# FFT mixing and a squared-ReLU FFN on one core: x cast one period ahead, first loads uncast on one queue, first transform over six PSUM banks

## Chip, core and metric

One core of a Trainium2 chip runs one program. The metric is device time in microseconds (us) of one execution; smaller is better.

## What is computed

x is 8 x 3008 x 256 in fp32. Along the 3008 positions each channel is transformed (real FFT), multiplied by a complex filter of 1504 + 1 frequencies per channel, and transformed back. The 24064 rows that come out go through a squared-ReLU FFN with 2048 hidden columns:

```python
X = np.fft.rfft(x, axis=1)
y = np.fft.irfft(X * (filt_r + 1j * filt_i)[None], n=3008, axis=1)
h = np.maximum(y.reshape(24064, 256) @ w_in, 0.0)
out = (h * h @ w_out).astype(np.float32)
```

## The kernel before

All matmuls are fp16 with fp32 sums. The FFT of length 3008 = 64 x 47 is done by constant matrices in stages, batch by batch.

- **Load and cast.** `load_x` (L139) brings a quarter of a batch, 96 x 2048 fp32, into one of two buffers; `cast_x` (called in `unit_a`) turns it to fp16 on VectorE (L186) in one of two buffers.
- **Stage A.** `unit_a`, 16 units a batch, four per quarter: one matmul of 512 columns (L196), copied from PSUM by ScalarE (even units, L201) or VectorE (odd, L203). After each quarter 384 KB go to the DRAM scratch dU (L205), in rows of 256 fp16 elements. `read_u` (L213) reads all of dU back in another order, in two transfers.
- **Stages B and P.** `unit_b`, 12 units: two matmuls (L219), and VectorE multiplies with the filter tile sF (L222). `unit_p`: four matmuls (L236), copied by ScalarE (L238); every third unit writes 384 KB to the scratch dZ (L241). `read_z` (L247) reads it back in four transfers.
- **Stage Y.** `unit_y`, 16 units of four matmuls (L259), copied to y by ScalarE or VectorE in turn (L266, L268).
- **FFN.** 47 groups of 512 rows, eight slots each. In a slot `ffn_g1` does the first matmul for two of 16 hidden tiles (L289) and the ReLU on ScalarE (L293), `ffn_g2` an eighth of the second matmul of the group before (L304), `ffn_sq` the square on VectorE (L297). `ffn_out` copies (L311) and stores (L313) a result every fourth slot. h2 (hidden values) has two buffers.

Engines work through their instructions in the order written; SyncE issues nearly all DMAs. That order is written out by hand. `fft_plan(b)` gives each unit of a batch a slot and one of two places in it: stage A in slots 0 to 7, the read of dU after slot 8, B and P in 13 to 25, the reads of z in 27, the loads of the next batch's first two quarters in 28, stage Y in 31 to 38. Batch 0 runs its plan alone, ahead of the FFN (the lead-in). Batch b from 1 to 7 starts its plan at the FFN slot in which the group that needs it lies 40 or 48 slots ahead (slots 0, 40, 88, 136 and so on, one period each), and each slot of the FFN then runs:

```python
ffn_g1(g, k)
run(work, s, 0)        # place 0
ffn_g2(g - 1, k)
run(work, s, 1)        # place 1
ffn_out(g - 1, k)
ffn_sq(g, k)
```

PSUM has eight banks: two for the FFT (`psF`), two tiles of two banks for the FFN's first matmul (`psH`), two for its second.

Constants and weights: sSA comes on SyncE, sSB, sSP and sSY on ScalarE's queue. The filter tile sF and both FFN weights come on GpSimd's queue, cast from fp32 to fp16 by the DMA (L170 to L179). At slot 12 of the lead-in VectorE copies sF's second half (L348, L349).

Of the kernel before, what the change touches and what calls it, by code (L numbers as in the profile page):

```python
# [86 lines left out]
def kernel(  # L87
# [29 lines left out]
    p_x16 = ctx.enter_context(tc.tile_pool(name="p_x16", bufs=2))  # L117
# [14 lines left out]

    def psF(name):
        return pps.tile([128, 512], F32, tag="psF", name=name, bufs=2)
# [4 lines left out]
    def load_x(b, c):  # L139

        t = p_x32.tile([96, 8, D], F32, tag="x32", name=f"x32_{b}_{c}")
# [8 lines left out]

    sSA = const.tile([94, 96], F16, name="sSA")
    nc.sync.dma_start(out=sSA, in_=dSA.ap())
    load_x(0, 0)
    load_x(0, 1)

    sSB = const.tile([128, NC, 128], F16, name="sSB")
    nc.scalar.dma_start(out=sSB, in_=dSB.ap().rearrange("p (a b) -> p a b", b=128))
    sSP = const.tile([128, NC, 2, 128], F16, name="sSP")
    nc.scalar.dma_start(out=sSP, in_=dSP.ap().rearrange("p (a t b) -> p a t b", t=2, b=128))
    sSY = const.tile([96, 94], F16, name="sSY")  # L160
    nc.scalar.dma_start(out=sSY, in_=dSY.ap())
# [3 lines left out]
    nc.gpsimd.memset(sF[32:64, 0, 0, :], 0.0)  # L165
    nc.gpsimd.memset(sF[96:128, 0, 0, :], 0.0)
    for c0, c1 in ((0, 12), (12, 24)):
        for r0, filt in ((0, filt_r), (64, filt_i)):
            v = filt[0:1504, :].rearrange("(k1 k2) d -> k1 k2 d", k2=47)
            nc.gpsimd.dma_start(out=sF[r0:r0 + 32, 0, c0:c1, :], in_=v[:, c0:c1, :])  # L170
            a = max(c0, 1)
            nc.gpsimd.dma_start(out=sF[r0 + 32:r0 + 64, 0, a:c1, :],
                                in_=v[:, 47 - a:47 - c1:-1, :])
    nc.gpsimd.dma_start(out=sF[32:33, 0, 0, :], in_=filt_r[1504:1505, :])

    sWin = const.tile([128, 2, DFF], F16, name="sWin")
    nc.gpsimd.dma_start(out=sWin, in_=moe_w_in.rearrange("(t r) j -> r t j", r=128))
    sWout = const.tile([128, NJT, 256], F16, name="sWout")
    nc.gpsimd.dma_start(out=sWout, in_=moe_w_out.rearrange("(jt r) c -> r jt c", r=128))  # L179
# [9 lines left out]
    def unit_a(b, a):  # L189

        c, i = divmod(a, 4)
        if i == 0:
            cast_x(b, c)
# [10 lines left out]
        if i == 3:  # L204
            nc.sync.dma_start(  # L205
# [3 lines left out]
    def read_u(b):  # L209
        ut = p_ut.tile([128, NC, D], F16, tag="ut", name=f"ut_{b}")  # L210
        v = dU[b].rearrange("(p s) d -> p s d", s=NC)
        for s0, s1 in ((0, 8), (8, 24)):
            nc.sync.dma_start(out=ut[:, s0:s1, :], in_=v[:, s0:s1, :])  # L213
# [102 lines left out]
    def fft_plan(b):  # L316
# [6 lines left out]
        for a in range(16):  # L323
            if a % 4 == 0 and a // 4 + 2 < 4:
                put(a // 2, 0, load_x, b, a // 4 + 2)
            put(a // 2, a % 2, unit_a, b, a)
# [74 lines left out]
```

## Time and profile before

| | |
|---|---|
| median of 3 runs | 897.73 us (896.83 to 898.89) |
| the profiled execution | 898.58 us |
| its span, first to last instruction | 896.80 us |
| lead-in, until the first FFN matmul | 91.47 us |
| TensorE busy | 792.4 us |
| VectorE, ScalarE, GpSimd busy | 479.1, 543.6, 7.9 us |

Times in the rows are us from the span's start unless marked ns. PE is TensorE's matmuls, PEld its weight loads, DVE VectorE, ACT ScalarE, POOL GpSimd, SP SyncE; a name with q (SPq) is the engine's queue issuing a DMA. `out<-in` names tiles; x32 after a shape is a count. An idle time is written with what ended it.

### The profile page before, as it was taken

The numbers are of one execution on the slowest core, as the hardware profiler recorded it, in microseconds if no ns is written. First come the engines' busy times: TensorE is split into PE (matmuls) and PEld (weight loads), VectorE is DVE, ScalarE is ACT, GpSimd is POOL, SyncE is SP. The second block draws the span as 40 slices with busy tenths as digits, with TensorE's granted clock in tenths as the row PEclk, the third lists the DMA queues.
The fourth block names the chain that finished last, engine by engine and source line by source line (L and its number), as shares of the span: only waits on it lengthen the run. The fifth ranks groups of instructions, "written<-read, shape, count | busy, mean of one in ns | idle before, by whom it ended". The sixth has DMA issues, their size and how long they took to land.

```text
span 896.8 us, 14010 instructions
## 1 busy us (share of the span) xinstructions
PE 792.4 (88%) x5952; PEld 552.6 (62%) x5952; DVE 479.1 (53%) x636; ACT 543.6 (61%) x695; POOL 7.9 (1%) x17
## 2 busy tenths in 40 slices
PE   1245799979998899979999799988999799999998
PEld 0023377657776577656776577765767567766666
DVE  1443765566654575456744566545744567443332
ACT  1112667756765667656776566755676567766664
POOL 3000000000000000000000000000000000000000
PEclk9999999999999999999999999999999999999999
DMA  9935533544353426243261433534162432411111
GB/s 243 226 116 148 157 124 126 146 129 141 115 151 99 151 80 182 66 129 130 89 194 43 133 137 122 143 107 152 71 182 65 128 130 89 124 36 37 36 47 49
DMA packets 90942, 107.01 MB, mean 119 GB/s; under 512 B 4296, under 2 KB 81032, under 8 KB 86664
## 3 DMA queue, kind: packets, MB, share of 16 engines
q1 hardware_dynamic: 86384, 100.11, 37.1%
q0 software_dynamic: 4096, 3.64, 2.5%
q10 hardware_dynamic: 400, 2.38, 0.9%
q8 instruction: 46, 0.75, 0.4%
q14 instruction: 16, 0.13, 0.0%
HBM read 59.94 MB, written 49.81 MB: 122 GB/s over the span
## 4 chain that ended last, share of the span: by engine, by line
PE 84%; DVE 6%; DMA 5%; issue 2%; ACT 2%; SPq 0%; DVEq 0%; ACTq 0%
PE psO L304 36%; PE psH L289 34%; PE psP L236 5%; DVE x L186 4%; DMA x<-in_x_dram 4%; PE psA L196 3%; PE psB L219 3%; PE psY L259 3%; DVE h L297 2%; ACT ze L238 1%; ACT h L293 1%; DMA dU<-u 1%; DVE u L203 1%; DMA ut<-dU 0%; DMA zt<-dZ 0%
## 5 line engine op out<-in xcount | busy, mean ns | idle before, releaser
L293 ACT ACTIVATE h<-psH 128x1024 f16<-128x1024 f32 x376 | 385.1, 1024 | 206.0 <-PE psH L289 203.7
L304 PE MATMUL psO<-sWout,h 128*128 128x256 f16 x3008 | 388.6, 272 | 0.0
L289 PE MATMUL psH<-yt,sWin 128*128 128x512 f16 (+7 forms) x1728 | 388.1, 352 | 0.2 <-DVE yt L268 0.2
L297 DVE TENSOR_TENSOR h<-h 128x1024 f16<-128x1024 f16 x376 | 258.0, 686 | 188.8 <-ACT h L293 188.8
L304 PEld LDWEIGHTS <-h 128*128 128x128 f16 x3008 | 291.5, 98 | 83.1 <-issue 6.9
L289 PEld LDWEIGHTS <-sWin 128*128 128x128 f16 x1728 | 159.8, 98 | 100.6 <-issue 2.0
L222 DVE TENSOR_TENSOR prod<-psB,sF 128x1024 f16<-128x1024 f32 x96 | 117.4, 1224 | 57.6 <-PE psB L219 56.6
L196 PE MATMUL psA<-x,sSA 94*96 94x512 f16 x128 | 51.4, 421 | 73.9 <-DVE x L186 72.4
L238 ACT CAST ze<-psP 128x512 f16<-128x512 f32 x96 | 56.2, 585 | 68.0 <-PE psP L236 68.0
L203 DVE CAST u<-psA 96x512 f16<-96x512 f32 x64 | 44.0, 687 | 71.6 <-PE psA L196 70.3
L201 ACT CAST u<-psA 96x512 f16<-96x512 f32 x64 | 36.9, 577 | 57.8 <-PE psA L196 56.8
L268 DVE CAST yt<-psY 128x376 f16<-128x376 f32 x64 | 35.2, 550 | 66.5 <-PE psY L259 66.5
L196 PEld LDWEIGHTS <-sSA 94*96 94x96 f16 x128 | 16.0, 130 | 81.7 <-DVE x L186 59.5
L236 PE MATMUL psP<-prod,sSP 128*128 128x256 f16 x384 | 63.0, 290 | 1.6 <-DVE prod L222 0.9
L311 ACT COPY ost<-psO 128x512 f32<-128x512 f32 x94 | 55.4, 589 | 5.8 <-PE psO L304 5.8
L219 PE MATMUL psB<-ut,sSB 128*128 128x256 f16 x192 | 38.9, 288 | 16.8 <-DMA ut<-dU 10.6
L259 PEld LDWEIGHTS <-zt 96*128 96x128 f16 x512 | 36.7, 102 | 24.6 <-DMA zt<-dZ 6.9
L186 DVE CAST x<-x 94x2048 f16<-94x2048 f32 x32 | 38.9, 1217 | 23.2 <-DMA x<-in_x_dram 23.2
L259 PE MATMUL psY<-sSY,zt 96*128 96x94 f16 x512 | 44.1, 213 | 8.1 <-DMA zt<-dZ 6.5
L236 PEld LDWEIGHTS <-sSP 128*128 128x128 f16 x384 | 39.8, 104 | 9.1 <-issue 1.4
L219 PEld LDWEIGHTS <-sSB 128*128 128x128 f16 x192 | 19.4, 101 | 41.1 <-issue 20.5
L266 ACT CAST yt<-psY 128x376 f16<-128x376 f32 x64 | 29.9, 468 | 10.4 <-PE psY L259 10.4
(16 smaller groups left out, 13.3 us busy)
## 6 DMA issues: line engine op xcount, KB each, us to landing
out_dram<-ost SPq DMA_DIRECT2D x94, 256.0 KB, 2.2
x<-in_x_dram SPq DMA_DIRECT2D x28, 768.0 KB, 9.1
dU<-u SPq DMA_DIRECT2D x32, 384.0 KB, 3.4
dZ<-ze SPq DMA_DIRECT2D x32, 384.0 KB, 2.3
zt<-dZ SPq DMA_DIRECT2D x32, 384.0 KB, 5.8
ut<-dU SPq DMA_DIRECT2D x8, 1024.0 KB, 6.1
ut<-dU SPq DMA_DIRECT2D x8, 512.0 KB, 3.7
x<-in_x_dram SPq DMA_DIRECT2D x4, 640.0 KB, 5.7
```

The lines of the kernel that those rows point to most:

```text
L186: nc.vector.tensor_copy(out=t, in_=x32s.pop((b, c))[0:94])
L196: nc.tensor.matmul(ps[0:96, :], sSA, x16s[(b, c)][:, 2 * i:2 * i + 2, :], start=True, stop=True)
L219: nc.tensor.matmul(ps[:, i * D:(i + 1) * D], sSB[:, 2 * p + i, :], uts[b][:, 2 * p + i, :], start=True, stop=True)
L222: nc.vector.tensor_mul(out=prod, in0=ps.rearrange("p (a d) -> p a d", d=D).unsqueeze(1).to_broadcast([128, 2, 2, D]), in1=sF[:, :, 2 * p:2 ...
L236: nc.tensor.matmul(ps[:, i * D:(i + 1) * D], sSP[:, 2 * p + i, v, :], prod[:, v, i, :], start=(v == 0), stop=(v == 1))
L238: nc.scalar.copy(out=zes[(b, c)][:, 2 * i6:2 * i6 + 2, :], in_=ps.rearrange("p (a d) -> p a d", d=D))
L259: nc.tensor.matmul(ps[:, 94 * jj:94 * jj + 94], zt[:, 4 * (g % 2) + jj, dt * 128:(dt + 1) * 128], sSY, start=True, stop=True)
L289: nc.tensor.matmul(ps[:, i, o:o + n], sWin[:, dt, jt * 128:(jt + 1) * 128], yts[b][:, dt, r:r + n], start=(dt == 0), stop=(dt == 1))
L293: nc.scalar.activation(out=h2[:, 2 * s:2 * s + 2, :], in_=ps, func=AF.Relu)
L297: nc.vector.tensor_mul(out=v, in0=v, in1=v)
L304: nc.tensor.matmul(pso[g][:, t % 2, :], h2s[g][:, jt, t * 128:(t + 1) * 128], sWout[:, jt, :], start=(jt == 0), stop=(jt == NJT - 1))
L311: nc.scalar.copy(out=ost, in_=pso[g])
```

## The change

- x is cast a period ahead: batch b+1's four casts stand in slots 27, 30, 33 and 36 (place 1) of batch b's plan, no longer in stage A; there are four fp16 buffers. The loads of its first two quarters move from slot 28 to slot 22; those of the last two follow the first two casts, in slots 27 and 30, and no longer lie in stage A. Batch 0's casts stay in stage A.
- In the lead-in all four quarters of x are loaded at once, the last two into the FFN's h2 buffers.
- sSB, the filters (as fp32, into the two y buffers), sSP and sSY follow on SyncE in this order; then, at slot 9, both FFN weights as fp32 into the h2 buffers. VectorE casts the filters, GpSimd the weights, in eight copies of 1024 columns.
- In the lead-in the writes of dU and its read go out on ScalarE's queue.
- In the lead-in the FFT's PSUM tiles rotate over six banks: two of `psF` and four of `psH`.

```diff
     p_x32 = ctx.enter_context(tc.tile_pool(name="p_x32", bufs=2))
-    p_x16 = ctx.enter_context(tc.tile_pool(name="p_x16", bufs=2))
+    p_x16 = ctx.enter_context(tc.tile_pool(name="p_x16", bufs=4))
     p_u = ctx.enter_context(tc.tile_pool(name="p_u", bufs=3))
...
+    banks = []
     def psF(name):
-        return pps.tile([128, 512], F32, tag="psF", name=name, bufs=2)
+        if not prologue[0]:
+            return pps.tile([128, 512], F32, tag="psF", name=name, bufs=2)
+        if not banks:
+            for k in range(2):
+                banks.append((pps.tile([128, 512], F32, tag="psF", name=f"{name}_{k}", bufs=2), None))
+            for k in range(2):
+                t = pps.tile([128, 2, 512], F32, tag="psH", name=f"{name}_h{k}", bufs=2)
+                banks.extend([(t, 0), (t, 1)])
+        t, i = banks.pop(0)
+        return t if i is None else t[:, i, :]
+    prologue = [True]
...
-    def load_x(b, c):
-        t = p_x32.tile([96, 8, D], F32, tag="x32", name=f"x32_{b}_{c}")
+    def load_x(b, c, pool=None, tag="x32"):
+        t = (pool or p_x32).tile([96, 8, D], F32, tag=tag, name=f"x32_{b}_{c}")
         if b + 1 < B:
...
     sSA = const.tile([94, 96], F16, name="sSA")
...
     load_x(0, 1)
+    load_x(0, 2, p_h2, "h2")
+    load_x(0, 3, p_h2, "h2")
     sSB = const.tile([128, NC, 128], F16, name="sSB")
-    nc.scalar.dma_start(out=sSB, in_=dSB.ap().rearrange("p (a b) -> p a b", b=128))
-    sSP = const.tile([128, NC, 2, 128], F16, name="sSP")
-    nc.scalar.dma_start(out=sSP, in_=dSP.ap().rearrange("p (a t b) -> p a t b", t=2, b=128))
-    sSY = const.tile([96, 94], F16, name="sSY")
-    nc.scalar.dma_start(out=sSY, in_=dSY.ap())
+    vSB = dSB.ap().rearrange("p (a b) -> p a b", b=128)
+    nc.sync.dma_start(out=sSB, in_=vSB)
     sF = const.tile([128, 2, NC, D], F16, name="sF")
-    nc.gpsimd.memset(sF[32:64, 0, 0, :], 0.0)
-    nc.gpsimd.memset(sF[96:128, 0, 0, :], 0.0)
+    f32s = []
     for c0, c1 in ((0, 12), (12, 24)):
+        t = p_y.tile([128, 12, D], F32, tag="yt", name=f"f32_{c0}")
+        if c0 == 0:
+            nc.gpsimd.memset(t[32:64, 0, :], 0.0)
+            nc.gpsimd.memset(t[96:128, 0, :], 0.0)
         for r0, filt in ((0, filt_r), (64, filt_i)):
             v = filt[0:1504, :].rearrange("(k1 k2) d -> k1 k2 d", k2=47)
-            nc.gpsimd.dma_start(out=sF[r0:r0 + 32, 0, c0:c1, :], in_=v[:, c0:c1, :])
+            nc.sync.dma_start(out=t[r0:r0 + 32, 0:12, :], in_=v[:, c0:c1, :])
             a = max(c0, 1)
-            nc.gpsimd.dma_start(out=sF[r0 + 32:r0 + 64, 0, a:c1, :],
-                                in_=v[:, 47 - a:47 - c1:-1, :])
-    nc.gpsimd.dma_start(out=sF[32:33, 0, 0, :], in_=filt_r[1504:1505, :])
+            nc.sync.dma_start(out=t[r0 + 32:r0 + 64, a - c0:12, :],
+                              in_=v[:, 47 - a:47 - c1:-1, :])
+        if c0 == 0:
+            nc.sync.dma_start(out=t[32:33, 0, :], in_=filt_r[1504:1505, :])
+        f32s.append(t)
+    sSP = const.tile([128, NC, 2, 128], F16, name="sSP")
+    nc.sync.dma_start(out=sSP, in_=dSP.ap().rearrange("p (a t b) -> p a t b", t=2, b=128))
+    sSY = const.tile([96, 94], F16, name="sSY")
+    nc.sync.dma_start(out=sSY, in_=dSY.ap())
     sWin = const.tile([128, 2, DFF], F16, name="sWin")
-    nc.gpsimd.dma_start(out=sWin, in_=moe_w_in.rearrange("(t r) j -> r t j", r=128))
     sWout = const.tile([128, NJT, 256], F16, name="sWout")
-    nc.gpsimd.dma_start(out=sWout, in_=moe_w_out.rearrange("(jt r) c -> r jt c", r=128))
+    def load_w():
+        w32 = p_h2.tile([128, 2, DFF], F32, tag="h2", name="win32")
+        nc.sync.dma_start(out=w32, in_=moe_w_in.rearrange("(t r) j -> r t j", r=128))
+        o32 = p_h2.tile([128, NJT, 256], F32, tag="h2", name="wout32")
+        nc.sync.dma_start(out=o32, in_=moe_w_out.rearrange("(jt r) c -> r jt c", r=128))
+        for k in range(4):
+            nc.gpsimd.tensor_copy(out=sWin[:, :, 512 * k:512 * k + 512],
+                                  in_=w32[:, :, 512 * k:512 * k + 512])
+        for k in range(4):
+            nc.gpsimd.tensor_copy(out=sWout[:, 4 * k:4 * k + 4, :], in_=o32[:, 4 * k:4 * k + 4, :])
+    def cast_f(k):
+        c0, c1 = 12 * k, 12 * k + 12
+        nc.vector.tensor_copy(out=sF[:, 0, c0:c1, :], in_=f32s[k])
+        nc.vector.tensor_copy(out=sF[0:64, 1, c0:c1, :], in_=sF[64:128, 0, c0:c1, :])
+        nc.vector.tensor_copy(out=sF[64:128, 1, c0:c1, :], in_=sF[0:64, 0, c0:c1, :])
...
         if i == 0:
-            cast_x(b, c)
             us[(b, c)] = p_u.tile([96, 8, D], F16, tag="u", name=f"u_{b}_{c}")
...
         if i == 3:
-            nc.sync.dma_start(
+            q = nc.scalar if prologue[0] else nc.sync
+            q.dma_start(
                 out=dU[b].rearrange("(m q) d -> q m d", q=96)[:, 8 * c:8 * c + 8, :],
...
         v = dU[b].rearrange("(p s) d -> p s d", s=NC)
+        q = nc.scalar if prologue[0] else nc.sync
         for s0, s1 in ((0, 8), (8, 24)):
-            nc.sync.dma_start(out=ut[:, s0:s1, :], in_=v[:, s0:s1, :])
+            q.dma_start(out=ut[:, s0:s1, :], in_=v[:, s0:s1, :])
         uts[b] = ut
...
         for a in range(16):
-            if a % 4 == 0 and a // 4 + 2 < 4:
-                put(a // 2, 0, load_x, b, a // 4 + 2)
+            if b == 0 and a % 4 == 0:
+                put(a // 2, 0, cast_x, b, a // 4)
             put(a // 2, a % 2, unit_a, b, a)
...
         if b + 1 < B:
-            put(28, 1, load_x, b + 1, 0)
-            put(28, 1, load_x, b + 1, 1)
+            for c in range(2):
+                put(22, 1, load_x, b + 1, c)
+            for c in range(4):
+                put(27 + 3 * c, 1, cast_x, b + 1, c)
+                if c < 2:
+                    put(27 + 3 * c, 1, load_x, b + 1, c + 2)
         for n in range(16):
...
     for r in range(41):
-        if r == 12:
-            for c0, c1 in ((0, 12), (12, 24)):
-                nc.vector.tensor_copy(out=sF[0:64, 1, c0:c1, :], in_=sF[64:128, 0, c0:c1, :])
-                nc.vector.tensor_copy(out=sF[64:128, 1, c0:c1, :], in_=sF[0:64, 0, c0:c1, :])
+        if r == 9:
+            load_w()
+            cast_f(0)
+            cast_f(1)
         run(plan0, r, 0)
         run(plan0, r, 1)
+    prologue[0] = False
```

## Rows read from the trace of the kernel before

**Rows 1.** The page, chain that ended last, share of the span by engine.

```profile
PE 84%; DVE 6%; DMA 5%; issue 2%; ACT 2%; SPq 0%; DVEq 0%; ACTq 0%
```

**Rows 2.** Stages: length; busy PE, PEld, DVE, ACT, POOL; clock, DMA share, GB/s.

```profile
16.30:41.50 25.20, 8.70 (x16) 2.28 (x15) 9.20 (x12) 4.65 (x8) 1.90 (x2) 1.00 1.16 224
...
51.27:77.25 25.98, 17.56 (x72) 9.85 (x72) 14.60 (x12) 7.03 (x12) 0.00 (x0) 1.00 0.18 73
...
83.07:91.47 8.40, 6.75 (x65) 5.28 (x66) 3.85 (x7) 3.78 (x8) 0.00 (x0) 1.00 1.12 271
91.47:896.80 805.33, 759.43 (x5803) 534.98 (x5800) 446.47 (x601) 526.88 (x666) 0.00 (x0) 1.00 0.37 112
```

**Rows 3.** Waits from 92 to 897 us: us in total, times, longest us.

```profile
PE psA L196 <- DVE x L186: 41.9, 27, 1.7
```

**Rows 4.** Events in order of time, third period: start, us, engine line.

```profile
177.92 0.42 PE L196 MATMUL psA<-x,sSA 94*96 94x512 f16 x1 [1.23 <-DVE x L186]
...
184.15 0.42 PE L196 MATMUL psA<-x,sSA 94*96 94x512 f16 x1 [1.64 <-DVE x L186]
```

**Rows 5.** Chain that ended last, in order of time: start, us, what.

```profile
41.50 6.00 DMA dU<-u
47.65 3.48 DMA ut<-dU
...
79.57 3.46 DMA zt<-dZ
```

**Rows 6.** The page, costliest groups: busy us, mean ns | idle before.

```profile
L293 ACT ACTIVATE h<-psH 128x1024 f16<-128x1024 f32 x376 | 385.1, 1024 | 206.0 <-PE psH L289 203.7
...
L222 DVE TENSOR_TENSOR prod<-psB,sF 128x1024 f16<-128x1024 f32 x96 | 117.4, 1224 | 57.6 <-PE psB L219 56.6
...
L203 DVE CAST u<-psA 96x512 f16<-96x512 f32 x64 | 44.0, 687 | 71.6 <-PE psA L196 70.3
L201 ACT CAST u<-psA 96x512 f16<-96x512 f32 x64 | 36.9, 577 | 57.8 <-PE psA L196 56.8
...
L186 DVE CAST x<-x 94x2048 f16<-94x2048 f32 x32 | 38.9, 1217 | 23.2 <-DMA x<-in_x_dram 23.2
```

**Rows 7.** Stage Y of the second period, slots 31 to 38, as rows 2.

```profile
248.81:265.13 16.32, 16.32 (x160) 11.95 (x159) 8.61 (x16) 12.08 (x18) 0.00 (x0) 1.00 0.56 155
```

**Rows 8.** Events in order of time, second period.

```profile
242.46 2.26 SPq L247 DMA_DIRECT2D zt<-dZ  x4
...
252.77 0.68 DVE L297 TENSOR_TENSOR h<-h 128x1024 f16<-128x1024 f16 x1
...
256.09 0.33 PE L259 MATMUL psY<-sSY,zt 96*128 96x94 f16 x4
```

**Rows 9.** DMA packets, 50 to 53 us, then 87 to 91 us.

```profile
DMA packets 204, 1.29 MB, mean 429 GB/s; under 512 B 18, under 2 KB 18, under 8 KB 76
...
DMA packets 140, 1.02 MB, mean 254 GB/s; under 512 B 16, under 2 KB 16, under 8 KB 16
```

**Rows 10.** DMA queues, 36 to 42, then 10 to 16 us: packets, MB, share.

```profile
q0 software_dynamic: 1221, 0.66, 77.6%
q1 hardware_dynamic: 1225, 0.62, 50.6%
...
q1 hardware_dynamic: 121, 0.86, 57.1%
...
q0 software_dynamic: 117, 0.06, 7.2%
```

**Rows 11.** Chain up to 95 us, two units of stages B and P.

```profile
58.02 0.59 ACT ze L238
...
58.66 0.59 PE psB L219 x2
59.24 0.87 PE psP L236 x4
...
60.77 0.59 PE psB L219 x2
```

## The prediction

> **What bounds the kernel now.** I read the page's chain first, then the span cut into stages, then who waited for whom, then events in order of time. The chain that ended last lies on TensorE for 84% [rows 1]. The cut shows two regimes [rows 2]. Up to 91.47 us the first transform runs alone, and TensorE is busy for 33 us (8.70 + 17.56 + 6.75). In the 805 us after that it is busy for 759, so what it still waits for is time on the path. The list of waits of that stretch names one thing of size: the stage-A matmuls wait 41.9 us in 27 waits for the cast of x on VectorE [rows 3]. One transform in order of time shows the shape: the cast begins when the VectorE queue reaches it, and TensorE stands 1.23 us before the first of its four pieces and 1.64 us before the next [rows 4], 6.1 us in four. Six such periods and 5 us in the first make the sum.
>
> The lead-in is a chain of transfers: x and stage A until 41.5 us, the last write of dU 6.00, its read back 3.48, stages B and P 26.0, the write and read of z 5.8, stage Y 8.4 [rows 2, 5].
>
> **Part 1, casts a period ahead (main part).** Six periods lose four waits each, batch 1 its three: -41.9 us. What comes back:
> - Batch 1's first eight slots have no second matmul, so without the cast ScalarE is close behind: a ReLU of 1.024 and a copy of 0.577 [rows 6] make 1.60 a slot, where TensorE has six matmuls of 512 columns, about 1.3. Of 5.0 I give back 0.5.
> - The casts go to slots 27, 30, 33, 36. VectorE is busy 8.61 of 16.32 us in slots 31 to 38 [rows 7], and 2 x 1.217 fit. What they delay is the square behind them in the queue, which nobody needs before the next group's second matmul, two slots or more away.
> - The cast in slot 33 also stands ahead of a copy of y, and it needs a load that SyncE issues in slot 27 behind four reads of z. In the second period the z reads are issued at 242.46 [rows 8]. The two loads moved to slot 22 (1.57 MB, 6.2 us at 254 GB/s [rows 9]), issued some 8 us before the last dZ is, push dZ and the z reads by at most 0.8. A transfer has about 2.3 us beside its bytes: the first read of dU back took 3.48 us [rows 5], of which 0.52 MB at 429 GB/s [rows 9] are 1.2. z needs 1.57 MB at 271 GB/s [rows 2] = 5.8, the load behind it 0.79 MB at 254 = 3.1: it lands at 242.5 + 0.8 + 2.3 + 5.8 + 3.1 = 254.5. VectorE gets there at 252.77 + 0.68 = 253.45 and waits 1.0; the copy of y ends at 254.5 + 1.22 + 0.55 = 256.3, and the matmul that needs its bank starts at 256.09 now [rows 8]. So I allow 0.3 a period, 6 x 0.3 = about 1.9. SyncE also stands in slot 27 until the cast has freed the buffer; behind it only a store of the output waits.
>
> Part 1: -41.9 + 0.5 + 1.9 = **-39.5** (-42 to -30).
>
> **Part 2, the lead-in up to stage B.** Loads go out on SyncE in the order sSA, x (3.15 MB), sSB (0.79), filters (3.08), sSP (1.57), sSY, then both FFN weights as fp32 (4.2) as soon as the casts of x(0,2) and x(0,3) have freed their buffers. At 254 GB/s the four pieces of x land from about 7 to 16 us. A piece takes VectorE about 4 us (cast 1.217, two matmuls, two copies of 0.687 with a matmul wait between [rows 6]), so stage A ends near 23 us instead of 41.5.
>
> That gain doesn't reach stage B, because of dU. Where two queues have work, the trace shows them served row for row: 36 to 42 us, 1221 packets of one queue and 1225 of the other; 10 to 16 us, 121 and 117 packets of two of three queues, though these move 0.86 and 0.06 MB [rows 10]. A queue of 512-byte rows beside one of 8 KB rows gets as many turns and a fourteenth of the bytes. dU goes out in 512-byte rows: 384 KB are 768 rows, four pieces are 3072, 192 turns of each of the 16 engines. Before, it shared a queue with x and met GpSimd's small rows; now it has ScalarE's queue and each row takes turns with the load queue. From about 12 us on, 192 turns there are some 5 of x, 8 of sSB, 100 of the filters (8 of 12 KB, 92 of 1 KB for the reversed rows), 8 of sSP, 6 of sSY, 16 of the first weight, 49 of the second. So the last dU lands when about 13.1 MB have gone through. At 260 GB/s (between 254 and 271 [rows 2, 9]) that is 50.4 us, plus 1 to land, plus 3.5 for the read: stage B starts near **55 us against 51.27, +3.7**. Bounds: at 429 GB/s, which a read of 128 long rows reached [rows 9], dU lands near 32 and stage B near 38 behind the filter casts; at 224 GB/s, the mixed stretch [rows 2], 63. I take 260, as the loads are of 96 and 32 partitions like x and not like the fast read. The filter casts (six passes of 3072 columns, at most 1.8 us each by the x cast's 1.217 for 2048) come in the shadow of dU; if dU were early they would set the start.
>
> [...]
>
> **Part 3, six banks in the first transform.** A stage-B unit takes 2.11 us now, as it waits for a bank until ScalarE has copied z; VectorE's product is 1.224 of it [rows 6, 11]. With banks to spare the product sets the pace, 1.27 with the gap. TensorE needs 1.3 for six matmuls, as four take 0.87 in this stage [rows 11]. 12 units plus 2.3 of head and tail: 17.6 us as the lower bound, 1.65 a unit if product and matmuls half alternate, 22. I take 18.5: -7.5.
>
> Little of it arrives. The moved loads of x(1,0) and x(1,1) enter SyncE's queue 14 us into stage B and occupy it to +21.5; the last dZ, issued at +18.5, lands at +23.3, the first z 3.46 later [rows 5]: stage Y starts at +26.9 (now +31.8, 83.07 - 51.27). Then the cast of x(1,2) stands in VectorE's queue before the copy of y 5. Its load follows the z reads: z until +29.9, x(1,2) lands +34, cast until +35.2; x(1,3) lands +37.1, cast until +38.3; three copies of y of 0.6 are left: **+40.1**, where the FFN now starts 40.2 after stage B (91.47 - 51.27). TensorE's extra banks let it run ahead but the FFN needs all of y. Part 3 is worth 0 (-5 to +5).
>
> GpSimd's eight weight casts end long before 95 us: they may take 30 us together at no cost (this trace has no copy on GpSimd).
>
> **Sum.** The profiled execution took 898.58 us (span 896.80). 898.58 - 39.5 + 3.7 + 0 = 862.8; it lay 0.85 above the median, so **862**. About 0.2% is what a measurement of this kernel can tell from no change.
>
> **Rivals.**
> - *dU isn't held up* (0.22): its writes pass between the loads, the filters bound. Loads to the filters with dU and its read are 10.1 MB, 39 us at 260, and the second half's passes up to 5.4: stage B near 43, 12 us earlier than forecast: 850. For it: nothing else asks for so many turns; against: the equal counts of rows 10.
> - *dU stands behind the whole load queue* (0.10), weights included: 12.8 MB at 260 = 49, dU 6, read 4.5: stage B at 60 to 63, total 867 to 870.
> - *The late load in slot 33* (0.10): if x(b+1,2) lands 2 us later than worked out, VectorE holds the copy of y, TensorE waits for its bank, and 2 us are lost in six periods and once in the lead-in: 862 + 14 = 876.
> - *Slower than before* (0.03): the same place, slot 33, priced at 1 us in seven places for each us late. From 5.2 us late the 36 us are given back; at 6 us it is 904. Against: the reads of z and the load behind them, 8.9 us of bytes, would have to take 15 where no other transfer of that size is in the queue.
>
> **How the numbers follow.** The forecast has 0.55, its own range 852 to 870. The range 845 to 876 takes in most of the first rival, the second and half of the third, and leaves out 2 in 10. Faster by over 0.2% 0.96, within 0.2% 0.01, slower 0.03.
>
> **What would show it.** Right: no wait of stage-A matmuls for the cast after the lead-in; the stage between stage A's end and stage B longer than 25 us, filled with dU packets equal in number to the load queue's; a product every 1.3 us in stage B; stage Y waiting for a cast. Wrong: stage B before 45 us, or TensorE waiting in slots 33 to 35 of each period.

## The result, and the profile after

The changed kernel takes 864.89 us in the median of four runs (860.49 to 869.45) against 898.04 on the same chip: ratio 0.9632 [0.9568, 0.9697]. Its profiled execution took 861.33 us, with a span of 859.6; the forecast for the profiled execution was 862.8. The total came out as forecast, its two halves did not: the lead-in (up to the first FFN matmul) shrank by 1.0 us where +3.7 was forecast, and the main part by 36.2 where 39.5 was.

The span of the changed kernel cut into stages (stage A; wait for dU; wait for the filters; stages B and P; then, after a gap for z, stage Y; main part), columns as in [rows 2]:

```profile
6.66:26.26 19.60, 8.40 (x16) 2.45 (x15) 10.11 (x12) 4.56 (x8) 0.00 (x0) 1.00 0.99 264
26.26:38.50 12.24, 0.00 (x0) 0.03 (x1) 3.67 (x3) 0.00 (x0) 0.00 (x0) 1.00 0.86 225
38.50:46.54 8.04, 0.59 (x2) 0.26 (x3) 3.67 (x4) 0.00 (x0) 0.00 (x0) 1.00 1.03 383
46.54:67.00 20.46, 12.20 (x70) 7.85 (x69) 14.40 (x12) 7.03 (x12) 8.00 (x8) 1.00 0.76 275
...
77.47:90.47 13.00, 6.14 (x65) 5.20 (x66) 6.13 (x10) 3.78 (x8) 0.00 (x0) 0.50 0.76 190
90.47:859.60 769.13, 755.89 (x5800) 535.20 (x5799) 439.21 (x597) 524.34 (x666) 0.00 (x0) 1.00 0.38 115
```

Against [rows 2]: stage A ends at 26 instead of 41.5; the first product starts at 46.54, where stage B started at 51.27 (its first product at 51.89); B and P take 20.46 instead of 25.98; but stage Y takes 13.0 instead of 8.40, and from the last write of z to the FFN it is 23.5 us (67.00 to 90.47) instead of 14.2 (77.25 to 91.47). So -4.7, -5.5 and +9.3 make -1.0.

In the main part the waits (columns as [rows 3]) no longer have the line of [rows 3]. In its place stand VectorE's cast, which waits for the load of x, and behind it stage Y, which waits for a copy of y:

```profile
DVE x L226 <- DMA x<-in_x_dram: 15.6, 6, 3.4
PE psY L300 <- DVE yt L309: 7.6, 6, 1.7
```

The second period in order of time, from the queue, VectorE and TensorE (start, us, engine and line), answers to [rows 8]:

```profile
227.76 0.34 SPq L282 DMA_DIRECT2D dZ<-ze  x1
232.58 2.62 SPq L288 DMA_DIRECT2D zt<-dZ  x4
...
243.73 1.22 DVE L226 CAST x<-x 94x2048 f16<-94x2048 f32 x1 [2.60 <-DMA x<-in_x_dram]
...
245.46 0.33 PE L300 MATMUL psY<-sSY,zt 96*128 96x94 f16 x4 [1.53 <-DVE yt L309]
```

This is slot 33. The cast waits 2.60 us where 1.0 was forecast, and TensorE 1.53 where 0.3 was allowed.

### The profile page after: what moved, and what is told of

Same layout as the page of the kernel before. It is cut to its first block, busy times and chain, and to the rows that moved or that the text cites. A ratio compares the mean times of both kernels' runs of the same rounds, so it can differ in the third digit from the quotient of the medians.

```text
span 859.6 us, 14006 instructions
## 1 busy us (share of the span) xinstructions
PE 783.2 (91%) x5952; PEld 551.2 (64%) x5952; DVE 479.7 (56%) x638; ACT 541.0 (63%) x695; POOL 8.8 (1%) x14
## 4 chain that ended last, share of the span: by engine, by line
PE 82%; DMA 12%; DVE 3%; ACT 2%; issue 1%; SPq 0%; DVEq 0%; ACTq 0%
PE psH L330 35%; PE psO L345 34%; DMA x<-in_x_dram 7%; PE psP L277 4%; PE psA L235 3%; DMA dU<-u 2%; PE psB L260 2%; PE psY L300 1%; DVE x L226 1%; DMA f<-in_filt_i_dram 1%; ACT h L334 1%; DMA dZ<-ze 1%; PE psP_h L277 1%; DVE prod L263 1%; ACT ze L279 1%
## 5 line engine op out<-in xcount | busy, mean ns | idle before, releaser
L263 DVE TENSOR_TENSOR prod<-psB,sF 128x1024 f16<-128x1024 f32 x84 | 102.9, 1225 | 42.2 <-PE psB L260 41.3
L279 ACT CAST ze<-psP 128x512 f16<-128x512 f32 x88 | 51.6, 586 | 66.3 <-PE psP L277 66.3
L242 DVE CAST u<-psA 96x512 f16<-96x512 f32 x59 | 40.5, 687 | 51.4 <-PE psA L235 50.6
L235 PE MATMUL psA<-x,sSA 94*96 94x512 f16 x118 | 45.1, 396 | 9.8 <-DVE x L226 9.8
L277 PE MATMUL psP<-prod,sSP 128*128 128x256 f16 x352 | 53.7, 276 | 0.0
L309 DVE CAST yt<-psY 128x376 f16<-128x376 f32 x59 | 32.2, 546 | 37.1 <-PE psY L300 37.1
L300 PE MATMUL psY<-sSY,zt 96*128 96x94 f16 x472 | 39.6, 208 | 9.5 <-DVE yt L309 7.6
L240 ACT CAST u<-psA 96x512 f16<-96x512 f32 x59 | 33.8, 573 | 11.3 <-PE psA L235 11.3
L260 PE MATMUL psB<-ut,sSB 128*128 128x256 f16 x168 | 32.1, 273 | 0.0
L307 ACT CAST yt<-psY 128x376 f16<-128x376 f32 x59 | 27.5, 467 | 2.7 <-PE psY L300 2.6
```

What stands on the lines that cost most here:

```text
L235: nc.tensor.matmul(ps[0:96, :], sSA, x16s[(b, c)][:, 2 * i:2 * i + 2, :], start=True, stop=True)
L260: nc.tensor.matmul(ps[:, i * D:(i + 1) * D], sSB[:, 2 * p + i, :], uts[b][:, 2 * p + i, :], start=True, stop=True)
L263: nc.vector.tensor_mul(out=prod, in0=ps.rearrange("p (a d) -> p a d", d=D).unsqueeze(1).to_broadcast([128, 2, 2, D]), in1=sF[:, :, 2 * p:2 ...
L277: nc.tensor.matmul(ps[:, i * D:(i + 1) * D], sSP[:, 2 * p + i, v, :], prod[:, v, i, :], start=(v == 0), stop=(v == 1))
L279: nc.scalar.copy(out=zes[(b, c)][:, 2 * i6:2 * i6 + 2, :], in_=ps.rearrange("p (a d) -> p a d", d=D))
L300: nc.tensor.matmul(ps[:, 94 * jj:94 * jj + 94], zt[:, 4 * (g % 2) + jj, dt * 128:(dt + 1) * 128], sSY, start=True, stop=True)
```

## The experiments

Each kernel was timed against the kernel before. "FFN at" is the start of the first FFN matmul in the profiled execution, "main part" the time from there to the end: 91.47 and 805.3 before, 90.47 and 769.1 after. One thing limits what "FFN at" can tell. Two later experiments (the changed kernel again, and loads in slot 18) have the changed kernel's lead-in unaltered, and their FFN starts at 91.87 and 94.22: the matmuls of stage P become twice as fast at about 55 us in the changed kernel's profile (four take 0.87 us at 51.98 and 0.45 at 57.12), in these by estimate near 57 (70 matmuls from 46.5 to 67 us take 12.77 us, where the changed kernel's took 12.20) and near 64 (the products come 1.83 us apart up to 62.65 and 1.3 from 64.87), and the first product of the last comes 1.5 us later. So differences of less than about 4 us in "FFN at", of one profile each, prove nothing by themselves.

### Each half by itself

**Casts ahead alone.** The kernel before with four fp16 buffers and the moved loads and casts; lead-in untouched.

```diff
...
-            cast_x(b, c)
...
-            put(28, 1, load_x, b + 1, 0)
-            put(28, 1, load_x, b + 1, 1)
+            for c in range(2):
+                put(22, 1, load_x, b + 1, c)
+            for c in range(4):
+                put(27 + 3 * c, 1, cast_x, b + 1, c)
+                if c < 2:
+                    put(27 + 3 * c, 1, load_x, b + 1, c + 2)
```

> The lead-in stays as before; only the casts (slots 27, 30, 33, 36), the moved loads and the four fp16 buffers are taken over. Theory (TensorE's 41.9 us of waits for the cast are the gain, part of it given back in slot 33): no stage-A wait for the cast, the FFN part as short as in the changed kernel, about 770 us from its first matmul, some 8 us of waits for VectorE's copies of y in six periods. In the lead-in the loads moved to slot 22 now lie ahead of the last dZ, and two casts hold the copies of y, so the first FFN matmul comes later than 91.5, near 96. Total about 868. Rival (the new lead-in carries part of the gain of the FFN part): 880 or more.

Measured: 871.91 us (870.34 to 873.36), ratio 0.9703 [0.9687, 0.9718]; FFN at 100.2, main part 770.5, six stops in slot 33 of 7.0 us together. The main part is within 1.4 us of the changed kernel's; the old lead-in pays 8.7 us for batch 1's loads and casts in its stages P and Y, where some 4.5 were expected.

**The lead-in alone.** The changed kernel, with the casts and loads of batches 1 to 7 put back into stage A.

```diff
+            if b:
+                cast_x(b, c)
             us[(b, c)] = p_u.tile([96, 8, D], F16, tag="u", name=f"u_{b}_{c}")
...
-                put(27 + 3 * c, 1, cast_x, b + 1, c)
...
```

> The lead-in of the changed kernel, with the casts and loads of batches 1 to 7 where they were before. Theory (the lead-in's own gain is eaten by the moved loads and casts): the last dZ lands some 2.3 us after its issue near 67, z 3.5 us later, stage Y isn't held: first FFN matmul near 80.5, the FFN part about 805, total about 887. Rival (the lead-in gains nothing by itself): first FFN matmul near 90, total about 896.

Measured: 889.88 us (889.22 to 892.62), ratio 0.9909 [0.9891, 0.9926]; FFN at 85.93, main part 804.9. Without batch 1's loads and casts in stages P and Y the new lead-in is worth 5.5 us in the profile, which is of the slowest of the four runs; in the medians the total is 8.7 us down (889.88 against 898.6). Of the 5.5 the changed kernel keeps 1.0. The 80.5 of the expectation was missed: the last write of z is issued at 70.41 instead of 67, as stage P's matmuls stay slow here to the end of the stage.

### The stop in slot 33

**Later casts.** The changed kernel with the last two casts three slots later.

```diff
-                put(27 + 3 * c, 1, cast_x, b + 1, c)
+                put((27, 30, 36, 39)[c], 1, cast_x, b + 1, c)
```

> The changed kernel with the third and fourth cast in slots 36 and 39 instead of 33 and 36. Theory (VectorE reaches the third cast before its load has landed and holds the copies of y): the 7.6 us of TensorE waiting for copies of y in six periods go, and in the lead-in the copies of y no longer wait for a load, first FFN matmul near 86.5. Total 10 to 12 us below the changed kernel's run on the same chip. Rival (the load is late for any slot, or the transfers of z are what is late): less than 3 us.

Measured: 851.39 us (850.94 to 853.81), ratio 0.9482 [0.9464, 0.95]. No line of stage Y waiting for VectorE is left in the main part, which takes 761.05:

```profile
88.55:849.60 761.05, 756.45 (x5800) 535.92 (x5800) 440.94 (x599) 523.89 (x666) 0.00 (x0) 1.00 0.38 116
```

It is 8.1 us shorter than the changed kernel's, the 7.6 us of the six stops and little else; the FFN starts at 88.55, 1.9 earlier. The load is as late as before; nobody waits for it.

**Earlier loads.** Why is the load late? SyncE's waits for the last write of z in the main part, in the kernel before and in the changed one (us in total, times, longest):

```profile
SPq L247 <- DMA dZ<-ze: 13.0, 7, 1.9
```

```profile
SPq L288 <- DMA dZ<-ze: 28.2, 7, 5.0
```

The two loads in slot 22 stand in the queue ahead of the last write of z. The experiment puts them ahead of an earlier one:

```diff
-                put(22, 1, load_x, b + 1, c)
+                put(18 if b else 22, 1, load_x, b + 1, c)
```

> The changed kernel with the loads of x(b+1,0) and x(b+1,1) in slot 18 instead of 22 from batch 1 on (the lead-in unchanged). Theory (the load behind the reads of z is late because those reads wait for the last write of z, and this stands behind the two loads of x: 28.2 us in seven waits in the changed kernel, 13.0 before): with the loads four slots earlier the wait for the write of z falls back to about 2 us a period, the cast in slot 33 waits 1 us instead of 2.6, TensorE's stops there fall from 7.6 us in six to 3 at most, FFN part 764 to 766, total 855 to 859. Rival (the reads of z and the load behind them take as long anyway): six stops of 1.3 us as before, total 861 to 868.

Measured: 856.7 us (854.29 to 857.23), ratio 0.9522 [0.9505, 0.954]. Its waits, of SyncE, VectorE and TensorE:

```profile
SPq L288 <- DMA dZ<-ze: 13.4, 7, 1.9
...
DVE x L226 <- DMA x<-in_x_dram: 4.0, 4, 1.2
...
PE psY L300 <- DVE yt L309: 0.3, 2, 0.2
```

The wait for the write of z is back at its old size, and the stops are gone with the casts where the change put them. Main part: 760.7 (94.22 to 854.90). The rival falls. So the two loads ahead of the last write of z make the load behind the reads late, and, with the experiment before, that late load makes the stop.

### The lead-in

**What held the loads.** SyncE's waits in the first 50 us of the changed kernel:

```profile
SPq L190 <- DMA dU<-u: 8.1, 1, 8.1
SPq L188 <- DMA dU<-u: 6.6, 2, 6.2
SPq L188 <- DMA x<-in_x_dram: 6.0, 1, 6.0
SPq L190 <- DMA x<-in_x_dram: 5.6, 1, 5.6
SPq L197 <- DMA ut<-dU: 4.9, 1, 4.9
```

L188 and L190 are loads of filters, L197 is sSP: none of them needs dU, ut or x. The trace names the semaphore that each DMA signals when it lands. In the first 45 us the DMAs of SyncE and ScalarE use eight, 100 to 102, 105 and 107 to 110, in turn: SyncE's have 100, 101, 102, 105, 107, 109, 100, 102, 107, 110 and so on, and the numbers left out, 108, 110, 101 and 105, are those of the four writes of dU. Each of these loads waits for the semaphore that it then uses itself, and none went out before the transfer that last had it had landed: on 110 the second write of dU landed at 24.59 and L190 was issued at 24.60, on 105 the fourth at 32.66 and L188 at 32.67, on 108 the first read of dU at 38.37 and sSP at 38.38. So the load queue did not run ahead of dU. The chain of the changed kernel up to 60 us (start, us, what) shows what that cost:

```profile
11.38 12.35 DMA dU<-u
...
26.26 6.39 DMA dU<-u
32.67 0.31 SPq L188
...
33.03 9.64 DMA f<-in_filt_i_dram
...
42.79 1.77 DVE sF L217
...
46.54 1.23 DVE prod L263
```

dU has landed at 32.65 and the first stage-B matmuls run at 38.5. The last filter load is issued only at 33.03, and the first product waits for the casts of both filter halves.

**Second filter half cast later.** Product 0 needs only the first half.

```diff
             cast_f(0)
+        if r == 17:
             cast_f(1)
```

> The changed kernel with the second half of the filters cast at slot 17 of the lead-in, after four products, instead of ahead of all. Theory (the product of unit 0 waited for the last filter load, at 42.7 us, and its casts until 46.5): unit 0 starts near 38.6, when dU has been read back, four units run while the load lands; stage B ends 5 to 6 us earlier, and so does the lead-in. Total 5 us below the changed kernel. Rival (dU sets the start of stage B, as forecast, or the transfers behind stage P set its end): no change within 2 us.

Measured: 867.83 us (865.42 to 872.12), ratio 0.9663 [0.9629, 0.9696]: no gain. The chain of this kernel:

```profile
33.69 5.62 DMA ut<-dU
39.33 7.97 DMA sSP<-cSP
```

Product 0 starts at 40.07, but sSP is issued only when the first read of dU has landed and holds stage P to 47.3. The wait moved to the next load held by a semaphore. Then the second half's casts stand between products 3 and 4, and product 4 starts at 57.36 (54.19 in the changed kernel); the FFN at 95.47. By estimate GpSimd's weight casts run beside them now (the weights are issued at 43.76 and 44.25, 1.0 us later than in the changed kernel, whose casts run from 51.32 to 60.62), and two of these copies take longer than the 0.95 us that each took there:

```profile
53.95 1.68 DVE L218 COPY sF<-sF 64x3072 f16<-64x3072 f16 x1
55.63 1.70 DVE L219 COPY sF<-sF 64x3072 f16<-64x3072 f16 x1
```

**And sSP ahead of that half.** As the last, with sSP loaded between the halves.

```diff
     for c0, c1 in ((0, 12), (12, 24)):
+        if c0:
+            nc.sync.dma_start(out=sSP, in_=dSP.ap().rearrange("p (a t b) -> p a t b", t=2, b=128))
...
```

> The changed kernel with the second filter half cast at slot 17, and sSP loaded ahead of that half. Theory (product 0 waits for the last filter load, and with only that wait gone stage P waits for sSP): product 0 near 40 to 41, no stop for sSP behind it, the FFN 3 to 6 us earlier than 90.5, total 859 to 862. Rival (the wait only moves once more: the second half lands later by the 5 us of sSP's load and its cast stops VectorE at product 6): FFN at 89 to 92, total 863.5 to 867.

Measured: 862.48 us (861.44 to 866.07), ratio 0.9606 [0.9585, 0.9627]; FFN at 91.98. Product 0 starts at 42.15 and stage P follows, then the casts of the second half stand in VectorE's queue and product 4 starts at 52.80 (54.19 in the changed kernel). The rival was right that this cast stops VectorE, but it does so at product 4 and by the 3.7 us of its own work (49.05 to 52.76), not by waiting for its load; in the median 2 us are left, less than the spread of the changed kernel.

**Writes of dU from GpSimd.** This should take them out of the turn of semaphores: in the trace of the kernel before, GpSimd's DMAs have others, 102 to 109, than those of SyncE and ScalarE.

```diff
-            q = nc.scalar if prologue[0] else nc.sync
+            q = nc.gpsimd if prologue[0] else nc.sync
```

> The changed kernel with the four writes of u in the first FFT issued by GpSimd instead of ScalarE. Theory (the loads on SyncE are held back because SyncE's and ScalarE's transfers take eight semaphores in turn, and a load waits for the write of u that last had its semaphore): with the writes out of that turn SyncE issues the filters without stops, all by 20 us, and they land by 45; but then the writes of u take turns with 13 MB of loads as the prediction had it, so that stage B starts late: near 50 to 55 instead of 38.5, and the FFN 5 to 10 us later: total 870 to 875. Rival (the order of issue hardly matters, the bytes do): SyncE issues as in the changed kernel, with stops of 6 to 8 us, or without them and product 0 stays at 45 to 47.5: total 863 to 867.

Measured: 860.31 us (859.27 to 862.88), ratio 0.9579 [0.9563, 0.9595]; product 0 at 38.42, stage P held for sSP until 45.8, FFN at 91.17. SyncE's waits in the first 50 us, the largest two:

```profile
SPq L197 <- DMA ut<-dU: 14.0, 1, 14.0
SPq L190 <- DMA x<-in_x_dram: 7.5, 1, 7.5
```

The waits for the writes of dU are gone, the filters are all issued by 23.6 (33.4 in the changed kernel), and the load after them waits 14 us for the read of dU: the semaphores hold the loads. The other half of my expectation, dU slowed by the loads, did not come: the last write took 7.17 us (6.39 in the changed kernel). But the test isn't clean there: on GpSimd's queue dU went out in other packets. From 8 to 37 us this queue has (packets, MB, share), first in this experiment, then ScalarE's in the changed kernel:

```profile
q0 software_dynamic: 448, 1.57, 17.0%
```

```profile
q10 hardware_dynamic: 3256, 2.05, 25.5%
```

That is 3.5 KB a packet on average against 0.6. How late dU would be with 512-byte rows beside a queue that does run ahead stays open.

**Two banks.** The changed kernel with the FFT over two PSUM banks in the lead-in.

```diff
-        if not prologue[0]:
+        if True:
             return pps.tile([128, 512], F32, tag="psF", name=name, bufs=2)
```

> The changed kernel with its first FFT over two PSUM banks, as before the change. Theory (the six banks save what the prediction says within stages B and P: 20.5 us in the changed kernel from product 0 to the last write of z, against 25.4 in the kernel before): product 0 stays near 46.5, the last write of z is issued near 72 instead of 67.0, the FFN starts near 95 instead of 90.5, total 869 to 870. Rival (the prediction's net figure: the loads and casts of batch 1's x eat the gain whatever the banks do): FFN still at 90.5 to 91.5, total 865 to 866.

Measured: 866.72 us (863.58 to 867.98), ratio 0.9637 [0.9614, 0.9659]; the last write of z issued at 71.94, FFN at 96.0. In the profile the four banks bring 4.3 us in B and P (24.8 from product 0 to the last write, against 20.5) and 5.5 at the FFN, as the theory had it; in the medians 1.8, inside the spread. But the changed kernel's matmuls in stage P turn fast at about 55 us, and here they are slow to the end (from 60 to 68 us TensorE is busy 5.68 us with 24 matmuls, in the changed kernel 3.66 with 26). In two other profiles with six banks (later casts, with 6.47 us for 29 there, and lead-in alone) they are slow to the end too, and B and P take 23.8 and 23.4, with units 1.9 us apart. So at like matmuls the banks are worth 1.0 to 1.4 us in B and P; the rest of the 4.3 goes with the faster matmuls. Whether the banks bring those about is not shown; no profile with two banks has them in B and P.

### Towards a better version

**All of it, first try.** Later casts (batch 1's in slots 33, 34, 39 and 40), sSP first, second half at slot 17, and batch 1's loads of x behind the last write of z.

```diff
-                put(22, 1, load_x, b + 1, c)
+                put(22 if b else 28, 1, load_x, b + 1, c)
...
+                s = (27, 30, 36, 39)[c] if b else (33, 34, 39, 40)[c]
```

> The changed kernel with sSP first and the second filter half cast at slot 17, batch 1's loads of x put behind the last write of z, and the casts of x later (slots 27, 30, 36 and 39, for batch 1 slots 33, 34, 39 and 40). Theory (three separate waits: filters and sSP, the last write of z behind two loads of x, and Y behind the casts): FFN near 82, FFN part 761 as with the late casts alone, total 842 to 846. Rival (the lead-in is bound by its bytes, only the casts matter): FFN at 87 to 89, total 849 to 852.

Measured: 852.77 us (852.35 to 853.2), ratio 0.9491 [0.9477, 0.9505]: a miss, level with the later casts alone; FFN at 90.31 where 82 was expected. The write of z lands in 2.3 us (6.9 in the changed kernel) and Y begins at 75.5 instead of 77.5, but then VectorE stands in Y again, and TensorE 4.05 us behind it:

```profile
83.34 1.22 DVE L227 CAST x<-x 94x2048 f16<-94x2048 f32 x1 [5.05 <-DMA x<-in_x_dram]
```

**Batch 1's casts behind Y.** The later casts and the loads behind the write of z, with batch 1's casts in slots 39 and 40 and in slots 3 and 5 of the FFN.

```diff
+            if b == 1 and a in (6, 10):
+                put(a // 2, 1, cast_x, b, a // 4 + 1)
...
-                put(22, 1, load_x, b + 1, c)
+                put(22 if b else 28, 1, load_x, b + 1, c)
...
+                s = (27, 30, 36, 39)[c] if b else (39, 40, None, None)[c]
```

> The changed kernel with the late casts (slots 27, 30, 36 and 39) from batch 2 on; batch 1's first two loads of x issued behind the last write and the reads of z (slot 28), its first two casts in slots 39 and 40, its last two in slots 3 and 5 of the FFN. Theory (Y of the first FFT is held only by the last write of z standing behind two loads of x and by casts that wait for loads): the last write of z issued near 70.6 lands in 2.3 to 2.8 instead of 5.4 to 6.9, Y from 76 on without a stop, the FFN near 84.5 (with the late casts alone 88.55), FFN part 761 to 762, total 847 to 849. Rival (with the loads of x behind the reads of z, batch 1's stage A now waits for them, as much as Y gained): FFN near 85, FFN part 765 or more, total 851 or more.

Measured: 848.33 us (847.7 to 849.75), ratio 0.944 [0.9426, 0.9454]; FFN at 85.37, main part 762.5: within a microsecond of the theory.

**And the loads let free.** The same with sSP first, the second half at slot 17, and the writes of dU from GpSimd (diffs above).

> The same, and besides sSP loaded ahead of the second filter half, that half cast at slot 17, and the writes of u in the first FFT issued by GpSimd. Theory (what held the filters and sSP was their issue behind the semaphores of the writes of u, not their bytes): sSP issued before 20 instead of 38.4, product 0 near 38.5 and stage P at once, the last write of z issued near 63 instead of 70.6, the FFN near 77 to 78, total 841 to 843. Rival (the bytes of the loads ahead of stage P bind: 12.2 MB by 46.5 us at 262 GB/s): products stop for the second filter half or sSP until 46 to 48 as before, the FFN at 83 to 85, total 847 to 849.

Measured: 845.65 us (843.96 to 846.36), ratio 0.9402 [0.9386, 0.9418], the fastest version; FFN at 82.18. That lies between the two expectations. Product 0 starts at 40.70, 2.2 us later than the theory had it; SyncE's wait for the read of dU, below, ends only at 39.96 (38.38 in the changed kernel). Then the casts of the second half stop VectorE for their own 3.7 us, and product 4 starts at 51.12. One of the last filter loads stands long behind the read of dU, but its cast follows product 3 without a wait, so this costs nothing that can be seen:

```profile
SPq L193 <- DMA ut<-dU: 16.1, 1, 16.1
```

### The spread of the changed kernel

Its runs lie as far apart as 860.5 and 869.5, those of the later casts within 3 us. So it was run again.

> The changed kernel once more, unchanged. Its four runs were 860.5 and 861.3, 868.5 and 869.5. Theory (the two pairs differ in the lead-in alone, where TensorE's granted clock once rose during stages B and P, fell in the wait for z and stayed low into the FFN's first slots): again 860 to 870 in two groups; a run of the upper group has its first FFN block at the same time or later and a longer first batch, and the periods from batch 2 on are as long in both. Rival (something that recurs in every period, such as the late load in slot 33, is longer in the upper group): periods of batches 2 to 7 longer by 1 us or more each.

Measured: 864.16 us (863.74 to 868.15), ratio 0.9624 [0.9602, 0.9647]; the profiled execution took 868.15. Neither was right. FFN at 91.87 explains 1.4 of the 6.8 us. The reads of z are 85.2, 99.2, 99.7, 99.4, 99.7 us apart from batch to batch in the first profile and 88.2, 99.2, 101.9, 99.4, 99.3 in this one: single periods are longer. The reads of batch 4 come 101.9 us after those of batch 3, and between them lies this (TensorE's event, then windows of 1 us with the columns of [rows 2]):

```profile
350.12 0.33 PE L300 MATMUL psY<-sSY,zt 96*128 96x94 f16 x4 [1.98 <-DVE yt L309]
```

```profile
349.00:350.00 1.00, 0.00 (x0) 0.00 (x0) 1.00 (x3) 0.00 (x0) 0.00 (x0) 1.00 0.78 201
350.00:351.00 1.00, 0.88 (x7) 0.50 (x7) 1.00 (x3) 0.00 (x0) 0.00 (x0) 0.79 0.73 228
351.00:352.00 1.00, 1.00 (x7) 0.45 (x6) 0.72 (x2) 0.05 (x1) 0.00 (x0) 0.50 0.11 38
352.00:353.00 1.00, 1.00 (x8) 0.76 (x7) 0.00 (x0) 1.00 (x2) 0.00 (x0) 0.50 0.00 0
353.00:354.00 1.00, 1.00 (x9) 0.76 (x8) 0.00 (x0) 0.34 (x1) 0.00 (x0) 0.51 0.00 0
354.00:355.00 1.00, 1.00 (x11) 0.52 (x9) 0.78 (x2) 0.58 (x1) 0.00 (x0) 1.00 0.00 0
```

After the stop in slot 33 the granted clock fell to 0.50 for 3.4 us. Around 163 us the same happened, there 0.6 us before the end of a stop of 3.01 us; in the main part of the first profile it did not happen. The stops themselves were longer, 11.0 us against 7.6. In sum the main part has 3.0 us more of busy TensorE and 2.4 more of idle. That the other long runs have the same cause is not shown, as they left no trace. The mean granted clock on record does not settle it: 0.982 in the two long runs of the changed kernel against 0.985 and 0.986 in the short ones, but 0.980 to 0.982 in the three runs of this experiment at 864. The spread fits in the main: five of the six kernels without the stop spread by less than 3 us and one (the lead-in alone) by 3.4, those with it by 3.0 (casts ahead alone) to 9.0.

## Why the prediction was right, step by step

**Part 1, the term removed.** Right, and somewhat small. With the stop in slot 33 away the main part is 761.05 and 760.7 in two kernels, 44 us below 805.3; I had 41.9 - 0.5. In the changed kernel 1.2 us of the difference lie in batch 1's first eight slots, which take 13.2 us instead of 18.9, where I took 4.5 off; the rest was not traced.

**Part 1, slot 33: the mis-sized term.** "So I allow 0.3 a period" measured 7.6 / 6 = 1.27. The mechanism and the place were right, and so was nearly all of the sum: from the issue of the z reads to the landing of the load it is 243.73 - 232.58 = 11.15 us, my terms gave 2.3 + 5.8 + 3.1 = 11.2. One term failed: that the two moved loads "push dZ and the z reads by at most 0.8". I reckoned the loads done before the last write of z came; it was issued at 227.76, and they landed at 228.23 and 230.93. From the issue of that write to the reads it is 4.82 us (227.76 to 232.58) instead of 2.38 before, 2.4 more. The 1.6 that I missed are VectorE's wait of 2.60 in place of 1.0, and 1.2 of them reached TensorE. The loads in slot 18 took the 2.4 away and the stop with them. The price that I gave in the rivals, 1 us lost for each late, was somewhat high: here 1.6 us late cost 1.2 more, and over the six periods, with 15.6 us of waits of VectorE and 7.6 of TensorE, it was about 0.6 for each.

**Part 2: wrong.** Stage B was to start near 55; its first matmuls started at 38.50 and the first product at 46.54. The row turns are in the trace where both queues have rows; the changed kernel from 29 to 31 us, columns as [rows 10] (q1 is SyncE's queue, q10 ScalarE's):

```profile
q1 hardware_dynamic: 346, 0.34, 67.4%
q10 hardware_dynamic: 327, 0.17, 33.0%
```

The first write of dU took 12.35 us and the last 6.39, where the last took 6.00 before [rows 5]. No row shows the 1 us that the sum has for its landing; the last row of that write ended at 32.27, and it had landed at 32.65. But the turns did not hold throughout. From 11.4 us, when the first write of dU is issued, to 16 us only the load queue has packets, 190 of them; why is not shown. And from 22 to 25 us nearly half of dU's 3072 rows pass with next to nothing beside them:

```profile
q10 hardware_dynamic: 1491, 0.75, 88.6%
q1 hardware_dynamic: 18, 0.02, 4.1%
```

SyncE stood in the longest of its waits then, until 24.60. What failed is the step "From about 12 us on, 192 turns there are" some of x, of sSB, of filters, of sSP and of the weights: it takes for granted that SyncE's queue always has the next load in it. It hadn't, since each load from the second filter piece on waited for a semaphore, which a write of dU held in three cases (14.7 us). So dU was through at 32.65, and the loads were late instead: the filters, which I had in dU's shadow, and their casts set the start. I could have seen it: GpSimd's queue in the kernel before has a filter load that waits for another filter load, with no data between them (both signal on semaphore 102 in the trace):

```profile
POOL sF L174 <- DMA sF<-in_filt_r_dram: 7.3, 1, 7.3
```

What came is half of the first rival ("the filters bound"), at 46.5 where I gave it 43, and my own mark of a wrong forecast, "stage B before 45 us". How late dU would have been beside a queue that did run ahead stays open, as said above.

**Part 3: the mechanism right, its size not.** "I take 18.5: -7.5" was 20.46, -5.5. I had 1.27 a unit; the first six products took 1.78 each (46.54 to 57.21), the next five 1.43 (to 64.35), with TensorE slow in the first part (below); in the profiles where it stays slow, six banks have units 1.9 us apart. The loss behind it came as I told it, and larger: the last write of z, 6.9 us from issue to landing where I had 4.8, behind the loads of x(1,0) and x(1,1), and the copy of y behind a cast that waits for its load. SyncE, VectorE and TensorE of the changed kernel in the lead-in:

```profile
67.00 0.34 SPq L282 DMA_DIRECT2D dZ<-ze  x1
74.04 2.21 SPq L288 DMA_DIRECT2D zt<-dZ  x4
```

```profile
85.01 1.22 DVE L226 CAST x<-x 94x2048 f16<-94x2048 f32 x1 [4.81 <-DMA x<-in_x_dram]
...
86.75 0.47 PE L300 MATMUL psY_h<-sSY,zt 96*128 96x94 f16 x4 [3.81 <-DVE yt L309]
```

The FFN starts 43.9 us after the first product, where I had 40.1 after stage B.

GpSimd's eight casts cost nothing here: 8.0 us in stage B and P, done 30 us before they are needed.

**The sum.** -1.0 - 36.2 against +3.7 - 39.5: an error of 4.7 us in the lead-in and one of 3.3 in the main part took each other off. The 4.7 is itself what two larger errors left: the first product 8.5 us before the 55 of the forecast, and 3.8 us more from there to the FFN. The sign and the size of the whole rest on [rows 3], and those were sound; that the total came within 3 us is luck. The marks that I had set show it better than the total: of the four for a right forecast two came (no wait of stage A for the cast, stage Y waiting for a cast) and two did not (12.24 us instead of over 25 between stages A and B, products 1.4 to 1.8 us apart instead of 1.3), and both marks of a wrong one came, TensorE's wait in slot 33 being the second.

## What to carry to other kernels

A moved load is to be followed past every small transfer behind it in its queue: two loads of 768 KB ahead of the last write of z cost its readers 2.2 us a period (28.2 - 13.0 us in seven waits), and four slots earlier they cost nothing that can be seen in the main part. A load order is only as good as its issue: look in the profile for DMAs that wait for a transfer they need nothing from, and count the semaphores (here eight for the DMAs of two engines) before reckoning that a queue runs ahead. A cast that may wait for a load should not stand ahead of work that TensorE needs at once: three slots later, when its load had landed, it made this kernel's main part 8.1 us shorter (10 us in the two profiles as a whole, 13.5 in the medians, which the changed kernel's spread blurs).

## What the runs showed of the hardware

- A stop of TensorE in a full stretch cost nearly its own length again. In the second profile of the changed kernel a stop of 1.98 us ended at 350.12, the granted clock went from 1.00 to 0.50 within a microsecond, and it stayed there for 3.4 us, in which eight second matmuls of the FFN took 1.91 us instead of 1.04: by estimate 1.7 us more, half of the 3.4. The length of the stop alone does not decide it: stops of 2.15 us (casts ahead alone) and 2.20 (sSP ahead) also had such a fall around their end, those of 1.7 us or less in the first profile had none, and neither had one of 2.63 us with the writes of dU from GpSimd:

```profile
445.35 0.33 PE L300 MATMUL psY<-sSY,zt 96*128 96x94 f16 x4 [2.63 <-DVE yt L309]
```

```profile
445.00:449.00 4.00, 3.65 (x36) 2.55 (x36) 3.16 (x7) 2.22 (x4) 0.00 (x0) 1.00 0.25 79
```

- In the lead-in the clock column reads 1.00 from the start, but the trace has its first record of a granted clock at 54.93 us (1.00), and four matmuls of stage P take 0.87 us at 52 us and 0.45 at 57, as the chain shows; then, with TensorE idle from 66 us on, the column falls to 0.50 at 68.6 and stays there through stage Y. So up to the first record the column does not tell the clock here, and neither does it in stages B and P of the kernel before, whose first record is at 95.19; there four matmuls take 0.87 [rows 11].

```profile
51.98 0.87 PE psP_h L277 x4
...
57.12 0.45 PE psP_h L277 x4
```

- The packets in which a transfer goes out differed with the queue: the same 1.57 MB of dU went out in 448 packets on GpSimd's queue, and in rows of 512 bytes on ScalarE's.
- Copies on VectorE took longer once, by estimate beside casts on GpSimd: with the second filter half cast at slot 17, VectorE's copies of 64 x 3072 fp16 took 1.68 and 1.70 us; with sSP ahead, where GpSimd was idle until 55 us, the same copies took 0.95 each at 50.84 and 51.81. VectorE's products, six of which ran beside GpSimd's casts in the changed kernel, kept their 1.21 to 1.22 us.
